# Another fixed order of the attention's tasks in front of a top-1 mixture of experts

## The chip, the cores and the metric

The kernel runs on one core of one Trainium2 chip. The metric is the device time of one execution in microseconds. A core has five engines that run their own instruction streams in order: TensorE (PE, with its weight loads shown apart as PEld), VectorE (DVE), ScalarE (ACT), GpSimd (POOL) and SyncE (SP, which issues transfers). They wait for one another through semaphores.

## The reference, cut to what matters

Causal softmax attention and a linear memory read-out, mixed by a gate per head (B=4 batches, H=8 heads, S=576 positions, D=64), are followed by a mixture of experts in which each of the 2304 tokens goes to one of 8 experts.

```python
scores = scale * np.matmul(q, k.transpose(0, 1, 3, 2))        # causal, softmax over the last axis -> a
local = np.matmul(a, v)
q_p = phi(q)                                                  # elu(q) + 1
mem_out = einsum(q_p, M_prev) / (einsum(q_p, z_prev) + 1e-06)
attn = g * mem_out + (1 - g) * local                          # g = sigmoid(beta), one per head
x = attn.transpose(0, 2, 1, 3).reshape(B * S, H * D)          # 2304 tokens of 512
e_idx = np.argmax(x @ w_gate, axis=1)                         # top-1 routing
for e in range(8):
    mask = e_idx == e
    out[mask] = gate_w[mask] * eom[mask, e] * (np.maximum(x[mask] @ w1[e], 0) @ w2[e])
```

## The kernel before

The attention works on 16 pairs of heads (g = 0 to 15, four pairs to a batch) and on five query tiles of each pair (qt = 0 to 4, the last of 64 rows). What it does to them is cut into 1181 named tasks, each bound to one engine. The function `job` writes them down; a string, `ORDER`, lists all 1181 names in a fixed order, and one loop issues them in that order. Each engine then does its own tasks strictly in the order in which it got them, and waits where the inputs of the next are not there yet. A few tasks may run on either of two engines: the copies out of PSUM and the casts carry `:ACT` or `:DVE` behind their name.

The names that the text needs, with the line at which the profile shows them:

- **SS** scores of a pair and query tile on PE (L570, for the last tile L557, `s` and `sd`); **M** mask and row maximum on DVE (L628, for the last tile L596, `st` and `nm`); **E** exponentials on ACT (L633, for the last tile L605, followed by a read of the accumulated row sum).
- **T** transposes of the probabilities on PE (L645, L614 and L616, into `pt`); **V** copies of them to SBUF (L492, `PT`), on ACT or DVE; **P** probabilities times values on PE (L680, `po`); **O** copies of these to SBUF (L492, `oT`), on ACT or DVE.
- **C** and **R** split query and key into a high and a low part (L461 ACT or DVE, L465 POOL). **ME**, **N1**, **N2** are the memory product (PE L736), its norm and its scaling (DVE L742, L743, L749); **MW** and **MC** its weights (PE L700, DVE L705).
- **PL** with **YL**, **XL** (PE L904, DVE L912 and L913, POOL L923) mix both parts for the last batch, half of the heads at a time. **RT**, **RK**, **Tgate**, **GP**, **GS**, **CA**, **CJ**, **CB**, **Tpos** are the routing of a batch: small reductions on DVE (L256 to L329 and L884 to L891), a ranking by matmul (PE L235 to L238, `rk`), a transpose of the gates (PE L308) and its copy (DVE L312). **Z** tasks prepare the weights of the expert that runs first (among them DVE L1002, PE L1062, ACT L1072).

PSUM holds four buffers for scores, two for transposes (`pt`) and two for everything else, so a transpose into `pt` also waits until the V copy of the one before the last is done. Behind the loop over `ORDER` the code is the same in both kernels: the last routing steps and the first expert's gemms, then the experts, from about 216 us to the end.

Of the kernel before, what the change touches and what calls it, by code (L numbers as in the profile page):

```python
# [54 lines left out]
T1_2_0 V1_2_0:ACT T1_2_1 M2_0_0 M2_0_1 M2_1_1 E2_0_1 TS0_0 F03 P0_256_0 V1_2_1:DVE E2_0_0 E2_1_1 T1_4 M1_3_1 F21 V1_4_0:ACT LM1 M2_1_0 M1_3_0 P0_256_1
C3:DVE F12 P1_0_0 E2_1_0 V1_4_1:DVE T2_0 load4 E1_3_0 E1_3_1 V2_0:DVE SS2_2 R3 M2_2_0 M2_2_1 O0_256:ACT O1_0:ACT SS2_3 T2_1 T1_3_1 load_v3 E2_2_0
V2_1:ACT M2_3_0 V1_3_1:ACT TS1_0 E2_3_0 SS2_4 T1_3_0 V1_3_0:ACT M2_3_1 MW1 F13 F04 E2_2_1 T2_2_0 T2_3_0 TS1_1 ranks M2_4_0 P1_256_0 C4:DVE E2_3_1 F22 MC1
V2_2_0:ACT SS3_1 M3_0_0 V2_3_0:ACT P1_256_1 T2_2_1 M3_1_0 M2_4_1 E2_4 V2_2_1:ACT E3_0_0 load5 F23 O1_256:DVE M3_0_1 T2_3_1 TS2_0 load6 E3_0_1 E3_1_0
V2_3_1:DVE SS3_2 ME0_0 M3_2_1 T2_4 E3_2_1 R4 M3_1_1 wgz V2_4_0:ACT N10_0 N20_0 V2_4_1:ACT F06 SS3_4 T3_2_1 T3_0 M3_2_0 ME0_1 F14 V3_0:ACT M3_4_0
V3_2_1:ACT SS4_1 M3_4_1 E3_2_0 N10_1 SS4_2 E3_1_1 N20_1 T3_1 T3_2_0 C5:ACT P2_0_0 P2_256_0 TS2_1 E3_4 M4_0_0 V3_1:ACT M4_0_1 F24 M4_2_1 G0_1 M4_2_0  # L60
V3_2_0:ACT O2_0:ACT E4_0_1 E4_0_0 T3_4 M4_1_1 E4_1_1 E4_2_1 P2_256_1 V3_4_0:DVE TS3_0 M4_1_0 O2_256:DVE T4_0 SS3_3 E4_1_0 load_v4 E4_2_0 V3_4_1:DVE
M3_3_0 ME0_4 C6:ACT V4_0:ACT T4_2_0 SS4_4 V4_2_0:ACT R5 N10_4 T4_2_1 R6 TS3_1 N20_4 M3_3_1 M4_4_0 V4_2_1:ACT T4_1 E3_3_0 M4_4_1 load7 E3_3_1 V4_1:ACT
ME0_3 SS4_3 E4_4 T3_3_1 V3_3_1:ACT T3_3_0 N10_3 V3_3_0:ACT N20_3 M4_3_0 F16 E4_3_0 M4_3_1 ME0_2 N10_2 TS4_0 F05 SS5_1 SS5_2 N20_2 F26 T4_4 M5_0_0
M5_0_1 E4_3_1 P3_0_0 V4_4_0:DVE P3_256_0 O3_0:ACT E5_0_0 load9 P4_0_0 E5_0_1 M5_1_0 G0_3 P3_256_1 load_v5 F15 C7:ACT M5_2_0 W0 O3_256:ACT T4_3_0
O4_0:ACT F07 V4_4_1:DVE F25 E5_1_0 R7 T4_3_1 PV0_2 M5_2_1 M5_1_1 PV0_1 SS5_4 V4_3_1:ACT E5_1_1 E5_2_1 V4_3_0:DVE T5_0 Y0_2 G0_4 V5_0:ACT E5_2_0 Y0_1
M5_4_0 SS5_3 G0_0 M5_4_1 LT0_0 load8 XD0_1 LC0_0:DVE T5_2_0 V5_2_0:ACT XD0_2 M5_3_1 T5_1 PV0_4 E5_4 M5_3_0 T5_2_1 SS6_2 SS6_1 V5_2_1:DVE F09 V5_1:ACT
E5_3_0 E5_3_1 Y0_4 OUT0_2 M6_0_0 LT0_1 F08 M6_2_1 LC0_1:ACT T5_4 load_v7 OUT0_1 E6_0_0 V5_4_0:ACT F19 M6_2_0 LM2 LS0 SS6_4 TS5_1 V5_4_1:ACT TS5_0
E6_2_1 F17 M6_1_0 TS4_1 T5_3_1 T5_3_0 LY0 XD0_4 M6_0_1 E6_0_1 LB0 G0_2 V5_3_1:ACT V5_3_0:ACT PV0_0 P4_256_0 M6_1_1 T6_2_1 F18 LA0 RT0_0 Y0_0 E6_1_1
E6_1_0 RT0_1 T6_0 SS7_1 XD0_0 P4_256_1 P5_256_0 O4_256:ACT V6_0:ACT V6_2_1:DVE M6_4_0 RT0_2 E6_2_0 C8:ACT R8 F27 RT0_3 RT0_4 M7_0_0 P5_0_0 P5_256_1
OUT0_4 T6_1 CA0 F28 E7_0_0 O5_0:ACT M6_4_1 E6_4 O5_256:DVE T6_2_0 load_v6 V6_2_0:ACT M7_0_1 M7_1_1 ME1_0 SS6_3 M7_1_0 SS7_3 load_v8 V6_1:ACT load10  # L70
# [4 lines left out]
F010 TS7_0 V7_4_0:ACT E8_1_0 F111 T8_0 N11_3 E8_2_0 GA0 N21_3 TS7_1 F110 V7_4_1:ACT M8_2_1 G1_1 M8_3_1 P6_256_0 E8_2_1 P7_0_0 P6_256_1 M8_3_0 V8_0:DVE
SS9_1 O6_256:ACT E8_3_1 F013 O7_0:DVE T8_2_1 T8_1 F210 V8_2_1:ACT F211 M9_0_0 M9_0_1 PV1_0 T8_2_0 E8_3_0 V8_1:ACT P7_256_0 Tgate40 M9_1_1 W1 E9_0_1
V8_2_0:ACT Y1_0 M9_1_0 XD1_0 P7_256_1 load12 E9_0_0 T8_3_0 O7_256:ACT G1_4 G1_3 E9_1_1 V8_3_0:ACT PV1_1 OUT1_0 E9_1_0 F113 CJ0 LM3 load_v9 PV1_2
T8_3_1 Y1_1 Y1_2 SS8_4 M8_4_0 T9_0 M8_4_1 PV1_3 LT1_0 C11:ACT V8_3_1:ACT XD1_1 SS9_3 SS9_2 E8_4 V9_0:ACT G1_2 Y1_3 OUT1_1 M9_3_1 M9_3_0 load_v10 R11
LT1_1 XD1_2 T9_1 V9_1:ACT E9_3_0 SS9_4 LC1_0:DVE LC1_1:DVE LS1 TS8_0 XD1_3 M9_2_1 T8_4 E9_3_1 M9_2_0 LY1 V8_4_0:ACT SS10_1 LB1 OUT1_3 RK0 Tpos10
V8_4_1:ACT OUT1_2 T9_3_1 E9_2_1 PV1_4 LA1 M10_0_0 T9_3_0 Y1_4 RT1_0 V9_3_1:ACT M10_0_1 T9_2_1 E9_2_0 RT1_1 Tpos20 M9_4_0 V9_2_1:ACT C12:ACT P8_256_0  # L80
P8_0_0 Tpos30 M10_1_1 M10_1_0 P8_256_1 Tpos40 M9_4_1 RT1_2 CB0 F213 E10_0_1 V9_3_0:ACT T9_2_0 E10_0_0 E10_1_0 V9_2_0:ACT O8_0:DVE T10_0 E9_4 RT1_3
E10_1_1 V10_0:ACT O8_256:DVE RT1_4 SS10_2 M10_2_1 M10_2_0 E10_2_1 SS10_3 TS9_1 ME2_0 M10_3_0 R12 N12_0 load_v11 RX1 T10_1 SS10_4 SEL0_3 V10_1:ACT
E10_3_0 SEL0_2 ZI T9_4 N22_0 V9_4_0:ACT G2_0 TS9_0 E10_2_0 ME2_3 M10_3_1 SS11_1 C13:ACT V9_4_1:DVE E10_3_1 N12_3 R13 XD1_4 T10_2_1 T10_3_0 N22_3
V10_3_0:DVE M10_4_0 M11_0_0 E11_0_0 V10_2_1:ACT P9_256_0 P9_0_0 P9_256_1 M11_1_0 O9_0:ACT TS8_1 G2_3 T10_2_0 load15 O9_256:ACT T10_3_1 OUT1_4 F015
M10_4_1 V10_2_0:ACT M11_0_1 V10_3_1:ACT M11_1_1 Tgate11 Tgate31 E11_1_0 E10_4 E11_0_1 E11_1_1 SEL0_1 ME2_1 N12_1 SS11_3 N22_1 SS11_4 T10_4 RK1
V10_4_0:ACT MW3 T11_0 M11_4_0 Tpos11 M11_3_0 load14 TS10_1 V10_4_1:ACT V11_0:ACT MC3 T11_1 M11_3_1 V11_1:ACT ME2_4 Tpos21 CA1 CJ1 CB1 SS11_2 M11_4_1
E11_4 SS12_1 E11_3_1 N12_4 N22_4 T11_4 ZC M11_2_1 E11_3_0 TS11_1 M11_2_0 Z1 Z2 Tpos31 load_v12 M12_0_0 Z3 Z4 G2_1 V11_4_0:DVE Z5 P11_0_0 TS11_0
O11_0:ACT P10_256_0 P10_0_0 P10_256_1 F115 Tpos41 Z6 Z7 E12_0_0 Tgate21 M12_0_1 Z8 Z9 Z10 V11_4_1:DVE O10_0:ACT O10_256:DVE TS10_0 T11_3_0 T11_3_1
V11_3_1:DVE E11_2_1 M12_1_0 M12_1_1 ZN ME2_2 E12_0_1 C14:ACT N12_2 V11_3_0:ACT Tgate41 N22_2 E11_2_0 SS12_3 W2 T11_2_1 V11_2_1:ACT T11_2_0 SEL1_3
SS12_4 E12_1_0 PV2_1 T12_0 load_v14 V11_2_0:ACT E12_1_1 V12_0:ACT M12_3_1 M12_3_0 F215 P11_256_0 G2_2 SEL1_4 M12_4_0 Y2_1 E12_3_1 E12_3_0 SS13_1  # L90
P11_256_1 M12_4_1 SEL1_2 T12_1 M13_0_0 T12_3_1 M13_1_0 O11_256:ACT M13_0_1 V12_1:ACT M13_1_1 E12_4 XD2_1 PV2_4 PV2_3 R14 Y2_4 E13_1_1 T12_3_0 E13_0_1
SS12_2 SS13_3 XD2_4 OUT2_1 OUT2_4 V12_3_1:ACT V12_3_0:DVE M12_2_1 G2_4 E13_1_0 GA1 E13_0_0 T12_4 Y2_3 V12_4_0:ACT E12_2_1 F014 LT2_0 M12_2_0 LT2_1
T13_0 F012 SEL1_1 XD2_3 V12_4_1:DVE T13_1 LC2_0:DVE LC2_1:ACT V13_0:DVE M13_3_0 LS2 E12_2_0 V13_1:ACT SS13_2 T12_2_0 T12_2_1 E13_3_0 V12_2_1:ACT LY2
P12_0_0 M13_3_1 TS12_0 SEL0_4 load_v13 V12_2_0:ACT M13_2_0 O12_0:ACT PV2_0 LB2 M13_2_1 E13_2_0 SS13_4 T13_3_0 PV2_2 Y2_0 F112 F114 T13_2_0 Y2_2
# [1709 lines left out]
```

## Time and profile before

| | |
|---|---|
| time, median of 3 runs | 468.69 us (468.49 to 468.74) |
| profiled execution | 468.34 us, of which its span is 466.3 us |
| granted TensorE clock, mean of the span | 0.996 |
| busy in the span | PE 456.7, PEld 354.8, DVE 284.9, ACT 262.4, POOL 271.1 us |
| the attention's tasks | from the start to about 202 us |
| experts | about 216 us to the end |

Busy time of PE counts pipelined matmuls with modelled ends, so 98% is not PE at its peak. An engine that waits and is not the last link of the chain costs nothing.

### The profile page before, as it was taken

The page shows a single profiled execution, that of the slowest core. Times are in us where ns is not written, and L with a number is a line of the kernel's source. Part 1 is how long each engine was busy: PE and PEld are TensorE (multiplying, and loading weights), DVE is VectorE, ACT ScalarE, POOL GpSimd, SP SyncE. Part 2 cuts the span into 40 slices and gives each one's busy share as a digit, 9 for nine tenths or more (in the row PEclk, how much of TensorE's full clock was granted, in tenths as well). Part 3 has the DMA queues.
Part 4 walks back from the last instruction along what each step waited for, and adds up shares of the span by engine and source line. Part 5 has one row for each costly group of instructions (what it writes and reads, how often), then busy time and mean ns, then how long its engine had stood idle before and what let it go on. Part 6 is the DMA issues. An engine that isn't in the chain of part 4 may idle for free.

```text
span 466.3 us, 10798 instructions
## 1 busy us (share of the span) xinstructions
PE 456.7 (98%) x3517; PEld 354.8 (76%) x3517; DVE 284.9 (61%) x851; ACT 262.4 (56%) x625; POOL 271.1 (58%) x274
## 2 busy tenths in 40 slices
...
GB/s 239 204 144 143 21 216 158 158 58 199 30 153 30 86 181 99 59 142 153 47 265 324 299 309 170 328 46 346 265 202 341 115 208 221 124 147 182 29 31 39
DMA packets 30119, 75.90 MB, mean 163 GB/s; under 512 B 4307, under 2 KB 4839, under 8 KB 30058
## 3 DMA queue, kind: packets, MB, share of 16 engines
...
## 4 chain that ended last, share of the span: by engine, by line
PE 88%; DVE 3%; issue 2%; POOL 2%; ACT 2%; DVEq 1%; POOLq 0%; ACTq 0%
PE py L1432 18%; PE h L1432 17%; PE po L680 10%; PE pt L645 8%; PE s L570 7%; PE me L736 4%; PE hp L1458 3%; PE cy L1601 3%; PE ch L1601 3%; PE sd L557 3%; PE pt L614 2%; PE px L1400 2%; PE he L1123 1%; PE pv L799 1%; PE pl L904 1%
## 5 line engine op out<-in xcount | busy, mean ns | idle before, releaser
L633 ACT ACTIVATE st<-st,nm 128x128 f32<-128x128 f32 (+3 forms) x128 | 71.4, 562 | 3.7 <-DVE nm L628 3.6
L1465 POOL TENSOR_TENSOR hl<-hT,hh 128x512 fp32r<-128x512 f32 x32 | 43.5, 1380 | 40.6 <-ACT hh L1464 40.5
L628 DVE CUSTOM_DVE_ANT_0 st<-s,mask 128x128 f32<-128x128 f32 (+3 forms) x128 | 58.2, 483 | 8.2 <-PE s L570 4.1
L1108 DVE CAST whi<-kept 128x1024 fp32r<-128x1024 f32 x32 | 26.0, 811 | 51.6 <-ACTq L1439 40.7
L465 POOL TENSOR_TENSOR lo<-qk,hi 128x1216 fp32r<-128x1216 f32 x15 | 42.1, 2805 | 24.7 <-ACT hi L461 19.5
L1111 DVE TENSOR_TENSOR wlo<-kept,whi 128x1024 fp32r<-128x1024 f32 x32 | 54.4, 1701 | 1.1
L492 ACT COPY PT<-pt 128x512 f32<-128x512 f32 (+2 forms) x89 | 45.2, 523 | 15.9 <-PE pt L645 13.8
L1432 PE MATMUL h<-whi,xh 128*128 (+1 forms) x136 | 53.9, 396 | 0.0
L1432 PE MATMUL h<-whi,xl 128*128 (+1 forms) x136 | 53.4, 393 | 0.0
L1432 PE MATMUL h<-wlo,xh 128*128 (+1 forms) x136 | 53.4, 392 | 0.0
L1432 PE MATMUL py<-whi,hh 128*128 (+1 forms) x128 | 51.9, 406 | 0.0
L1432 PE MATMUL py<-whi,hl 128*128 (+1 forms) x128 | 50.2, 392 | 0.3 <-POOL hl L1465 0.3
L1432 PE MATMUL py<-wlo,hh 128*128 (+1 forms) x128 | 50.2, 392 | 0.0
L680 PE MATMUL po<-PT,v 128*64 128x320 f32 (+4 forms) x480 | 49.1, 349 | 0.8 <-ACT oT_hT L492 0.4
L645 PE MATMUL pt<-ident,st 128*128 128x128 f32 x320 | 48.0, 280 | 0.4 <-ACT st L633 0.4
L1464 ACT CAST hh<-hp 128x512 fp32r<-128x512 f32 x32 | 19.1, 598 | 50.6 <-PE py L1432 50.6
L1445 ACT ACTIVATE h<-h 128x1024 f32<-128x1024 f32 x17 | 17.5, 1029 | 47.9 <-PE h L1432 47.9
L680 PEld LDWEIGHTS po<-PT,v 128*64 128x64 f32 x480 | 29.6, 137 | 17.7 <-issue 2.8
L1411 POOL TENSOR_TENSOR xl<-x,xh 128x512 fp32r<-128x512 f32 x16 | 21.7, 1358 | 34.3 <-issue 19.0
L645 PEld LDWEIGHTS pt<-ident,st 128*128 128x128 f32 x320 | 35.2, 142 | 7.8 <-ACT st L633 2.5
...
L1432 PEld LDWEIGHTS h<-whi,xh 128*128 128x128 f32 x136 | 25.5, 188 | 6.0 <-ACT h L1445 0.3
...
## 6 DMA issues: line engine op xcount, KB each, us to landing
...
```

What stands on the lines that cost most here:

```text
L465: G.tensor_tensor(c["lo"][:, TQ:], c["raw"][:, TQ:], f32(c["hi"])[:, TQ:], op=ALU.subtract)
L492: (A.copy if e == "ACT" else V.tensor_copy)(dst(), src())
L570: T.matmul(c()["ss", q][j], l[r, lc], m[r, KC:KC + w], start=(a == 0), stop=(a == 2))
L628: V.tensor_tensor_reduce(st[:, :w], c()["ss", qt][j], mask[:, 512 - w:512], -SCALE, 3.0e38, ALU.add, ALU.min, negm()[:, i:i + 1])
L633: A.activation(st, st, AF.Exp, bias=c()["negm"][:, i:i + 1], scale=-1.0, accum_out=sums()[:, qt, 2 * p + j:2 * p + j + 1])
L645: T.transpose(pt[:, (m * k1 + i) * P:(m * k1 + i + 1) * P], st[:, i * P:(i + 1) * P], ident)
L680: T.matmul(po[64 * j:64 * j + 64, qs - q0:q1 - q0], vt[:, k, 64 * j:64 * j + 64], PT[:, j, k, qs:q1], start=(k == 0), stop=(k == kn - 1))
L1108: join((A.copy if eng is A else eng.tensor_copy)(whi[:, e % 2, c, :], raws[e, c]))
L1111: join(eng.tensor_tensor(wlo[:, e % 2, c, :], raws.pop((e, c)), f32(whi[:, e % 2, c, :]), op=ALU.subtract))
L1432: i = T.matmul(o[n % nh], l[:, z], m[:, n * 512 + part.start:n * 512 + part.stop], start=(c == 0 and k == 0 and n < nh), stop=(c == 3 and ...
L1465: G.tensor_tensor(hl[:, z], hT[:, z], f32(hh)[:, z], op=ALU.subtract)
L1601: i = apart(T.matmul(o[w * q:w * q + w], x[:, z:z + w], wide[b][:, m + size * q:m + size * q + size], start=(j == 0), stop=(j == len(todo) ...
```

## The change

The string `ORDER` is replaced by another order of the same 1181 tasks; no task is added, removed or altered. It was looked for by a search that lengthens tasks at random and lets two-operand tasks of VectorE and GpSimd exclude each other. The first row of the string and the start of its second are the same; behind them a name stands 7.7 places from where it stood, on average. 48 tasks change between ACT and DVE: 26 go from DVE to ACT and 22 from ACT to DVE, so that ACT has 140 of these tasks in place of 136 and DVE 44 in place of 48. Two rows of the string, before and after:

```diff
-E7_1_1 RX0 N11_0 E7_0_1 C9:ACT T6_4 N21_0 V6_4_0:ACT E7_1_0 PV0_3 M6_3_1 E6_3_1 M6_3_0 P6_0_0 Y0_3 V6_4_1:DVE TS6_0 E6_3_0 T7_0 O6_0:DVE M7_3_0 M7_3_1
-R9 TS6_1 V7_0:ACT SS7_2 ME1_4 N11_4 E7_3_0 T6_3_1 T7_1 E7_3_1 SS7_4 V7_1:ACT N21_4 M7_2_0 Tgate10 E7_2_0 V6_3_1:ACT M7_2_1 ME1_2 G1_0 N11_2 SS8_1
+SS7_3 load10 N21_0 RX0 T6_4 C9:ACT M7_3_0 TS6_0 M6_3_1 PV0_3 V6_4_0:ACT V6_4_1:DVE R9 Y0_3 P6_0_0 E7_0_1 T7_0 TS6_1 E6_3_1 M7_3_1 O6_0:ACT M6_3_0
+T6_3_1 E7_1_0 E7_1_1 V6_3_1:ACT E7_3_1 Tgate10 ME1_4 N11_4 SS7_2 N21_4 T7_1 SS7_4 V7_1:ACT M7_2_1 M7_2_0 ME1_2 V7_0:ACT SS8_1 E7_3_0 F29 T7_3_0 N11_2
```

In these rows T6_3_1 stood behind SS7_2 and ME1_4 on PE; now it stands directly behind T7_0.

**ACT, 188 to 191 us.** The rows are ACT's around the copy of `pxe` (task ZY, four rows). Before:

```order
L633 ACTIVATE st15_3_0_3209,sums3_2473<-st15_3_0_3209,nm15_3003 128x512
L492 COPY PT0_127<-pt14_2_0_3243 128x3x128
L1072 COPY star0_2910<-pxe_3252 128x128
...
L1072 COPY star3_3160<-pxe_3252 128x128
L492 COPY PT0_127<-pt14_2_1_3226 128x3x128
L492 COPY oT3_hT_2774<-po15_512_3271 128x64
L492 COPY oT3_hT_2774<-po15_0_3284 128x128
L633 ACTIVATE st15_2_0_3241,sums3_2473<-st15_2_0_3241,nm15_3003 128x384
```

Now:

```order
L492 COPY PT0_127<-pt14_2_0_3220 128x3x128
L492 COPY PT1_128<-pt15_1_0_3230 128x2x2x128
L1072 COPY star0_2979<-pxe_3252 128x128
...
L1072 COPY star3_3166<-pxe_3252 128x128
L633 ACTIVATE st15_2_0_3248,sums3_2465<-st15_2_0_3248,nm15_3000 128x384
L492 COPY oT3_hT_2780<-po15_512_3273 128x64
L633 ACTIVATE st15_2_1_3250,sums3_2465<-st15_2_1_3250,nm15_3000 128x384
L633 ACTIVATE st15_3_0_3269,sums3_2465<-st15_3_0_3269,nm15_3000 128x512
L492 COPY oT3_hT_2780<-po15_128_3298 128x128
```

The copies V14_2_1 (`pt14_2_1`) and O15_0 (`po15_0`) have left ACT for DVE. On PE the product P15_128, which writes over the buffer that O15_512 reads, stood directly behind P15_0 and P15_512; now four matmuls of 320 columns (P14_256, first part) stand between.

**DVE, 134 to 136 us.** The rows are DVE's around M11_4 (L596, `st11_4`), whose exponential feeds the transpose T11_4. Before:

```order
L628 ISA st11_3_1_2363,nm11_2231<-s11_3_1_2303,mask_138 128x512
L628 ISA nm11_2231 128x1
L323 TENSOR_REDUCE ps1_2347<-pos1_2346 128x5
L884 TENSOR_REDUCE addc1_2377<-oha_85 128x8
L887 TENSOR_TENSOR cnt_90<-cnt_90,addc1_2377 128x8
L891 CAST cntb_91<-cnt_90 128x8
L596 ISA st11_4_2344,nm11_2231<-sd11_4_1_2317,maskd_139,nm11_2231 128x288
```

Now:

```order
L320 TENSOR_TENSOR pos1_2339<-rk1_2325,oha_85 128x40
L596 ISA st11_4_2332,nm11_2228<-sd11_4_1_2303,maskd_139,nm11_2228 128x288
L596 ISA nm11_2228 128x1
L705 COPY mz3_1867<-mw3_2334 64x4x16 x2
L628 ISA st11_3_1_2356,nm11_2228<-s11_3_1_2192,mask_138 128x512
L628 ISA nm11_2228 128x1
L323 TENSOR_REDUCE ps1_2340<-pos1_2339 128x5
L884 TENSOR_REDUCE addc1_2364<-oha_85 128x8
```

M11_4's second half now stands ahead of M11_3_1 and of the routing's counting (L323, L884, and L887 and L891 further down).

**PE and DVE, 194 to 199 us.** PE's rows of the last pair's transposes, before:

```order
L308 MATMUL gp0_3337<-ident_77,og0_1540 5x128
L645 MATMUL pt15_3_0_3339<-ident_77,st15_3_0_3209 128x128 x4
L904 MATMUL pl0_1_3351<-rzt_136,oT3_hT_2774 128x160 x2
L645 MATMUL pt15_3_1_3354<-ident_77,st15_3_1_3267 128x128 x4
L308 MATMUL gp1_3369<-ident_77,og1_2278 5x128
L645 MATMUL pt15_2_0_3371<-ident_77,st15_2_0_3241 128x128 x3
```

Now, with DVE's rows of the same place behind them:

```order
L308 MATMUL gp0_3339<-ident_77,og0_1497 5x128
L904 MATMUL pl0_1_3347<-rzt_136,oT3_hT_2780 128x160 x2
L645 MATMUL pt15_3_0_3355<-ident_77,st15_3_0_3269 128x128 x4
L645 MATMUL pt15_3_1_3364<-ident_77,st15_3_1_3309 128x128 x4
L308 MATMUL gp1_3371<-ident_77,og1_2276 5x128
L645 MATMUL pt15_2_1_3381<-ident_77,st15_2_1_3250 128x128 x3
```

```order
L913 TENSOR_TENSOR yl0_1_3373<-pl0_1_3347,rr3_3141 128x320
L270 SCALAR_TENSOR_TENSOR oha_85<-mx2_3352,wt2_3362 128x40
L492 COPY PT1_128<-pt15_3_1_3364 128x4x128
L286 TENSOR_TENSOR wt2_3362<-lg2_2099,oha_85 128x40
L312 COPY gs1_3385<-gp1_3371 5x128
```

The product PLl0_1 (`pl0_1`) now comes directly behind GP0, without T15_3_0 between them, and the copy V15_3_1 (`PT1<-pt15_3_1`), which ACT did, is now DVE's, between L270 and L286.

## Rows read from the trace of the kernel before

**Rows 1.** The page: busy time, share of the span and instructions of each engine.

```profile
PE 456.7 (98%) x3517; PEld 354.8 (76%) x3517; DVE 284.9 (61%) x851; ACT 262.4 (56%) x625; POOL 271.1 (58%) x274
```

**Rows 2.** Busy time by stretch: bounds and length in us, engines, granted clock, DMA.

```profile
70.00:100.00 30.00, 30.00 (x308) 23.48 (x307) 27.21 (x104) 26.66 (x73) 17.27 (x15) 1.00 0.36 122
...
195.00:200.00 5.00, 4.38 (x54) 3.60 (x52) 4.83 (x27) 2.63 (x7) 2.33 (x4) 1.00 0.20 56
...
sum 193.00, PE 191.73 PEld 150.54 DVE 167.81 ACT 156.16 POOL 114.65; mean PE 17.43 PEld 13.69 DVE 15.26 ACT 14.20 POOL 10.42
```

**Rows 3.** PE's waits, whole span: line, releaser, us in total, times, longest.

```profile
PE po L680 <- ACT oT_hT L492: 0.4, 1, 0.4
PE pt L645 <- ACT st L633: 0.4, 1, 0.4
PE s L570 <- DVE nm L628: 0.3, 1, 0.3
PE py L1432 <- POOL hl L1465: 0.3, 1, 0.3
PE po L680 <- DVE gs L312: 0.3, 1, 0.3
PE rk L235 <- DVE oha L270: 0.2, 1, 0.2
```

**Rows 4.** Timeline, 188 to 190 us: start, us, instruction [idle before, its releaser].

```profile
188.71 0.77 ACT L1072 COPY star<-pxe 128x128 f32<-128x128 f32 x4 [0.75 <-PE pxe L1062]
...
189.34 0.53 ACT L492 COPY PT<-pt 128x384 f32<-128x384 f32 x1
...
189.71 0.44 ACT L492 COPY oT_hT<-po 128x64 f32<-128x64 f32 x2
...
190.03 0.55 PE L680 MATMUL po<-PT,v 128*64 128x128 f32 x6 [0.41 <-ACT oT_hT L492]
```

**Rows 5.** Timeline, 134 to 137 us.

```profile
134.81 0.22 DVE L884 TENSOR_REDUCE addc<-oha 128x8 f32<-128x40 bf16 x1
...
135.34 0.51 DVE L596 CUSTOM_DVE_ANT_0 st<-sd,maskd,nm 128x288 f32<-128x288 f32 x1
...
135.98 0.78 ACT L605 ACTIVATE st<-st,nm 128x576 f32<-128x576 f32 x1 [1.09 <-DVE nr L742]
...
136.90 0.20 PEld L614 LDWEIGHTS pt<-ident,st 128*128 128x128 f32 x2 [0.22 <-ACT st L605]
```

**Rows 6.** Timeline, 138 to 139 us: the weight load of P10_256.

```profile
138.56 0.74 PEld L680 LDWEIGHTS po<-PT,v 128*64 128x64 f32 x8 [0.32 <-DVE zw L1002]
```

**Rows 7.** Timeline, 195 to 199 us: the end of the attention.

```profile
195.57 0.57 PEld L904 LDWEIGHTS pl<-rzt,oT_hT 128*128 128x128 f32 x4 [0.35 <-DVE yl L913]
...
196.22 0.60 PE L645 MATMUL pt<-ident,st 128*128 128x128 f32 x4
...
197.41 0.74 POOL L923 TENSOR_TENSOR xa<-x,yl 128x256 f32<-128x256 f32 x1 [1.08 <-DVE yl L913]
...
197.47 0.73 DVE L286 TENSOR_TENSOR wt<-lg,oha 128x40 f32<-128x40 f32 x1
...
198.13 0.27 DVE L312 COPY gs<-gp 5x128 f32<-5x128 f32 x1
...
198.46 0.55 PE L680 MATMUL po<-PT,v 128*64 128x128 f32 x6 [0.27 <-DVE gs L312]
```

**Rows 8.** Timeline, 81 to 83 us: around T7_0.

```profile
81.44 0.58 ACT L492 COPY PT<-pt 128x512 f32<-128x512 f32 x1
...
82.41 0.72 ACT L633 ACTIVATE st<-st,nm 128x512 f32<-128x512 f32 x1
82.46 0.44 PE L645 MATMUL pt<-ident,st 128*128 128x128 f32 x2
```

**Rows 9.** DVE's copies of `pt`, whole span: ns min/median/max, first and last start.

```profile
L492 DVE COPY PT<-pt x23: 406/681/693, 9.4 to 178.8; 128x512 f32<-128x512 f32 x13, 128x256 f32<-128x256 f32 x5, 128x384 f32<-128x384 f32 x5
```

More of the change, by code (lines that the diff above doesn't have):

```diff
@@ L55 @@
[L55 to L70, printed above, removed]
@@ L75 @@
[L75 to L90, printed above, removed]
@@ L91 @@
[L91 to L94, printed above, removed]
@@ L103 @@
-P15_512_0 fetch4 P15_0_0 TL2_0 G3_0 O15_512:ACT O15_0:ACT P15_128_0 P14_256_0 E15_2_0 O15_128:DVE E15_2_1 P14_256_1 TL0_0 W3_1_1 W3_1_2 PLl1_1 LA2
-E15_3_1 W3_1_3 O14_256:ACT YLl1_1 XLl2_0 PLl4_1 PLl3_0 YLl4_1 GP0 T15_3_0 TL1_1 V15_3_0:ACT XLl1_1 XLl4_1 TL4_1 YLl3_0 PLl0_1 T15_3_1 GS0 RT2_0 GO0
-RT2_1 RT2_2 RT2_3 GP1 T15_2_0 YLl0_1 RT2_4 Tgate12 GS1 V15_3_1:ACT OL4 RX2 GO1 RK2 V15_2_0:ACT CA2 Tpos12 Tgate32 Tpos22 Tgate22 CJ2 T15_2_1 Tpos32
-Tgate42 V15_2_1:ACT GA2 CB2 Tgate52 P15_384_0 O15_384:ACT P15_256_0 Tpos42 Tgate62 TL0_1 TL3_0 XLl3_0 XLl0_1 PLl3_1 G3_3 SEL2_0 OL1 O15_256:ACT SEL2_3
```

68 lines of the change are left out of this document (54 added, 14 removed).

## The prediction

> **What bounds the kernel now.** I read the page's first part, then busy time by stretch, then PE's waits, and last the timeline at each place where something starts late. The page has PE busy for 98% of the span, every other engine for 76% or less [rows 1]. In the attention, which is all that the change touches, PE is busy 191.73 of the 193.00 us from 12 to 205 us [rows 2]; the one stretch where it is not is 195 to 200 us, with 4.38 of 5.00, where the last pair's work runs out and little is left to fill gaps. PE's waits of the whole span, as far as the view names them, are six of 0.2 to 0.4 us, 1.9 us in all, one of which (L1432, 0.3 us) lies in the experts, behind the change [rows 3]. So the order can win about 1.6 us of listed waits, and lose as much as it likes. Behind the attention PE goes on without a listed wait up to that one of L1432, so a microsecond won or lost before 202 us should arrive at the end.
>
> A wait that the matmul side does not list can still be there: PE's busy time has modelled ends, so a short wait is covered by the end of the matmul before it. The weight loads show such places; I use them as bounds.
>
> **What the change does.** The same instructions run, so PE's work is the same; only waits, and the changes of tile shape, can differ. I went through PE's rows in the new order, and for each counted what its releaser's engine has ahead of it. Four places carry the sum.
>
> *P15_128 at 190 us.* It writes into the buffer that the copy O15_512 reads. On ACT that copy stood behind the four rows of ZY (from 188.71) and V14_2_1 (0.53 us from 189.34), so it began at 189.71 and PE started at 190.03 after a wait of 0.41 [rows 4]. Now V14_2_1 is on DVE and PE has four matmuls of P14_256 ahead of P15_128. An exponential has taken V14_2_1's place ahead of the copy, so the copy is about as late as before; the gain comes from the four matmuls. Their price is not in these rows apart, but six matmuls of 128 columns take 0.55 there, so four wider ones are at least 0.37 us (estimate). Between nothing (the copy is later still) and the whole wait of 0.41 and a little that the modelled end covers, 0.6, I take −0.45.
>
> *T11_4 at 137 us.* Its releaser is the exponential E11_4, which began at 135.98, after M11_4's second half on DVE (135.34, 0.51 us); ahead of that DVE did L884 (0.22 us from 134.81) and two more small rows, 134.81 to 135.34, 0.53 us in all [rows 5]. These rows now stand behind M11_4, and so does M11_3_1. The load wait is 0.22 us [rows 5] and the two waits of this kind in the list are 0.4 and 0.3 [rows 3]. Bounds 0 and −0.7, taken −0.4, the longer of the listed ones.
>
> *P10_256 at 139 us.* Its load waited 0.32 us for Z2 on DVE [rows 6], with no matmul wait listed. In the new order Z2 is no longer the last to come. Bounds 0 and −0.32, taken −0.15.
>
> *T6_3_1 at 83 us, a new wait.* SS7_2 and ME1_4 no longer lie between T7_0 and T6_3_1. By the old times T7_0's second transpose is done about 82.46 + 2 x 0.11 = 82.68, with 0.11 us a transpose from 196.22, where four take 0.60 with a modelled end and the next row of PE came 0.43 us later [rows 7, 8]. The exponential E6_3_1 has a copy (0.58 from 81.44) and one exponential of a 128-column tile ahead of it, which with its overlap takes about what the 256-column one took there, since both leave its start near 82.41; it lasts 0.72 [rows 8], so it would be done near 83.1: 0.45 us late. If ACT comes to this place earlier than before, nothing is late. Bounds 0 and +0.5, taken +0.25.
>
> *The end, 195 to 199 us.* PLl0_1 waited for YLl3_0 with T15_3_0 in front of it, and its load still showed 0.35 us [rows 7]. Now T15_3_0 comes behind it, so its four transposes, 0.43 us, no longer cover: +0.43 there. But those transposes then fall behind, into the room of the waits that followed: RK2's for L270 (0.2, [rows 3]) and P15_384's for the copy GS1 (0.27, at 198.46, [rows 7]). GS1 itself hangs on DVE. There L286 took 0.73 us from 197.47, most of it beside POOL's L923 (197.41 to 198.15) [rows 7]; the copy V15_3_1 (up to 0.69 us, [rows 9]) now goes ahead of it. If L286 was merely held up by POOL's addition, the copy fills the hold, L286 runs in a short time once POOL is done, and GS1 starts where it did, near 198.13. If not, GS1 comes 0.69 later. The Trainium skill, "SBUF — State Buffer", section "Who interferes with whom", says that a VectorE instruction with two SBUF inputs contends with a GpSimd instruction that reads SBUF and that the loser blocks fully, while one with at most one SBUF input does not; by that the hold is real and the place costs nothing, and without it the sum below would be 0.5 us worse. I go by the row, since L286 ended within 0.05 us of POOL's end. Bounds −0.3 (both later waits filled) and +0.5, taken +0.1.
>
> *Small things.* At other places I count short waits that go (ME3_0 behind ZR, the ME tasks of batch 1) and short ones that come (P6_256, T12_3_1, T15_2_1 for its `pt` buffer); no row shows any of them as a PE wait, so they lie between −0.6 and +0.6, taken −0.35, as I count more that go. PE has two changes of tile shape fewer, at the most a transpose's slot each, 0 to −0.2, taken −0.1.
>
> The 48 tasks that change engine cost nothing where neither engine is waited for: ACT was busy 156.16 and DVE 167.81 of 193.00 us [rows 2]. A copy of 512 columns takes 0.58 on ACT [rows 8] and up to 0.69 on DVE [rows 9]; ACT gets four such tasks more. The cover is ACT's idle time, which was 3.3 us of 30 between 70 and 100 us [rows 2].
>
> Sum: −0.45 − 0.4 − 0.15 + 0.25 + 0.1 − 0.35 − 0.1 = **−1.1 us**. The profiled execution took 468.34 us, 2.0 us more than its span and 0.35 less than the median of 468.69; I take the difference from the median, 467.6 us. A difference under 0.2%, 0.94 us, is about what a measurement can't tell from none.
>
> **The rivals.**
> - *The waits are given back: same, 468.5.* PE is so nearly without waits that any order will have a few late inputs of its own. For it: T6_3_1, and PLl0_1 without cover, are new waits that I can already point at. If only the terms with listed waits at 190 and 137 us go (−0.85) and the new ones come larger than taken (+0.5 at T6_3_1, its upper bound, and +0.25 at the end, half of its bound), the change is −0.1; with the small things in balance at −0.1 it is −0.2. Against it: the waits that go are measured, and the new ones only counted.
> - *ACT falls behind between 70 and 100 us: slower, 469.9.* ACT is busy 26.66 of 30 us there [rows 2]. If the four copies that it got, 4 x 0.58 = 2.3 us, fall in this stretch and the exponentials run late by more than the transposes' lead, PE loses what ACT can't catch up. It decides from the point where this stretch's idle time of 3.3 us no longer lies where the added copies do; with 2.3 us lost and the 1.1 won it ends at 468.69 + 1.2 = 469.9. Against it: DVE has 2.8 us idle in that stretch too, and tasks move both ways.
> - *PE is not the bound: faster, 466.* The weight loads are busy only 150.54 of 193.00 us [rows 2], so 42 us could hide starved PE time that the modelled ends cover, and then an order can win several microseconds. With twice the short waits that I count gone, −2.5 us, it is 466.2. The Trainium skill, "Perfetto Trace Analysis", section "Identifying the Most-Contended Engine", says that matmul busy share is no good measure of how near TensorE is to its limit, and names the share of the weight loads instead; by that TensorE has 22% of headroom here. Against it: a transpose every 0.11 us keeps its pace through most of the attention.
> - *The order does not do what it was looked for.* Two-operand tasks kept apart would shorten DVE rows like L286; if DVE is not waited for at those places, nothing comes of it. That is inside "same".
>
> **How the numbers follow.** The forecast, that the sum holds within what its terms leave open to the better side, −0.9 to −1.8 us, has 0.40; given back in part or in whole, −0.9 to +0.9, 0.38; slower through ACT, above +0.94, 0.14; PE not the bound, below −1.8, 0.08. The forecast's own range is 466.9 to 467.8. The first and the last case are faster by over 0.2%: faster 0.48, same 0.38, slower 0.14. The range leaves out the lower end of the last case and the upper part of the slower one, 2 in 10 together: 466.5 to 469.4.
>
> **What would show it.** PE without a wait at P15_128 and T11_4; T6_3_1's load released by ACT's exponential, late by up to 0.5 us; PLl0_1's load wait near 0.8; L286 of the third batch short, behind a copy; the experts' first L1432 about 1 us earlier than 216.4. The prediction is wrong if PE's list names waits at places not above, if ACT's idle time between 70 and 100 us is gone while PE loses there, or if the experts start earlier and the end does not.

## The result: 1.1% slower, and on more than one level

| | time, us, median (range, runs) | ratio, 95% interval |
|---|---|---|
| before | 468.59 (468.41 to 468.74, 4) | |
| changed | 473.79 (472.06 to 476.30, 4) | 1.0111 (1.0075 to 1.0148) |

The forecast was 467.6 in a range of 466.5 to 469.4. The changed kernel's four runs fall into two groups, 472.06 and 472.08, and 475.50 and 476.30, where before's lie within 0.33 us. The profiled execution is one of 472.06, with a span of 470.3 us.

The page's first part of the changed kernel, as [rows 1], and two of its stretches and their sum, as [rows 2]:

```profile
PE 457.7 (97%) x3517; PEld 355.6 (76%) x3517; DVE 287.5 (61%) x847; ACT 263.4 (56%) x629; POOL 271.5 (58%) x274
```

```profile
40.00:70.00 30.00, 28.38 (x293) 21.52 (x291) 25.97 (x86) 26.14 (x72) 20.19 (x17) 1.00 0.33 112
70.00:100.00 30.00, 29.72 (x298) 23.74 (x298) 27.39 (x105) 26.61 (x74) 15.54 (x14) 1.00 0.41 134
...
195.00:200.00 5.00, 4.38 (x34) 3.34 (x30) 4.16 (x19) 1.36 (x5) 2.18 (x4) 1.00 0.03 7
...
sum 193.00, PE 189.87 PEld 150.16 DVE 170.07 ACT 156.49 POOL 115.34; mean PE 17.26 PEld 13.65 DVE 15.46 ACT 14.23 POOL 10.49
```

From 12 to 205 us TensorE is busy 189.87 us in place of 191.73, and the stretch that lost most, 40 to 70 us, is one of which the prediction says nothing. ScalarE between 70 and 100 us is as full as before (26.61 against 26.66). TensorE's waits, as [rows 3], with the one before the first score left out:

```profile
PE pt L645 <- ACT st L633: 1.8, 2, 1.4
...
PE rk L235 <- DVE oha L270: 0.8, 1, 0.8
PE pl L904 <- DVE yl L913: 0.5, 1, 0.5
PE s L570 <- DVE nm L628: 0.3, 1, 0.3
PE py L1432 <- POOL hl L1465: 0.3, 1, 0.3
PE h L1432 <- POOL xl L1411: 0.3, 1, 0.3
PE pt L645 <- ACT PT L492: 0.2, 1, 0.2
```

4.2 us in seven lines, against 1.9 in six. Two are new and large: 1.4 us for an exponential and 0.8 us for the routing's `oha`. The timeline of the changed kernel from 58 to 63 us shows the first of them from its root, in the order of time:

```profile
58.39 2.76 POOL L465 TENSOR_TENSOR lo<-qk,hi 128x1216 fp32r<-128x1216 f32 x1 [0.86 <-ACT hi L461]
...
58.86 2.91 DVE L520 SCALAR_TENSOR_TENSOR phi<-qk,phi 128x576 f32<-128x576 f32 x1
...
61.70 0.28 DVE L628 CUSTOM_DVE_ANT_0 st<-s,mask 128x128 f32<-128x128 f32 x1
...
62.07 0.40 ACT L633 ACTIVATE st<-st,nm 128x128 f32<-128x128 f32 x1 [1.90 <-DVE nm L628]
...
62.62 0.33 PE L645 MATMUL pt<-ident,st 128*128 128x128 f32 x1 [1.40 <-ACT st L633]
```

F25 (L520, the last step of elu(q) + 1 for pair 5; both operands lie in SBUF) came up on VectorE 0.47 us after GpSimd had begun R7 (L465). It took 2.91 us, where L520 otherwise takes 0.75, and was done 0.62 us after R7. I call that a hold: an instruction stays unfinished until another engine's is done. Behind F25 on VectorE stood M5_0_0 (61.70), whose exponential (62.07) feeds the transpose T5_0 on TensorE (62.62). In the old order F25 went first, from 58.84 to 59.57, and R7 ran its 2.85 us from 59.38. Before, from 58 to 60 us:

```profile
58.84 0.73 DVE L520 SCALAR_TENSOR_TENSOR phi<-qk,phi 128x576 f32<-128x576 f32 x1
...
59.38 2.85 POOL L465 TENSOR_TENSOR lo<-qk,hi 128x1216 fp32r<-128x1216 f32 x1 [2.91 <-ACT hi L461]
```

The second wait looks the same, at the last ranking:

```profile
206.50 1.47 DVE L270 SCALAR_TENSOR_TENSOR oha<-mx,wt 128x40 bf16<-128x40 f32 x1
206.51 1.40 POOL L923 TENSOR_TENSOR xa<-x,yl 128x256 f32<-128x256 f32 x2
...
208.03 0.19 PE L235 MATMUL rk<-oha,upper 128*128 128x40 bf16 x1 [0.84 <-DVE oha L270]
```

L270 takes 0.19 us alone, and took 0.55 at this place in the old order. Where the time went, read from TensorE's rows of both traces: GP0 came 2.57 us later (197.32 against 194.75), GP2 2.81 (204.34 against 201.53), the last ranking 3.65 (208.03 against 204.38), the first L1432 3.65 (220.03 against 216.38), and the span is 4.0 longer. Of the 2.57, 0.56 were there before the two orders differ (T0_3_1 at 12.31 against 11.75 us); two further profiles of the same kernel have that row at 12.14 and 11.72, so it is no part of the change.

### The profile page after: what moved, and what is told of

Read it like the earlier page. It is cut to its first block, busy times and chain, and to the rows that moved or that the text cites. A ratio compares the mean times of both kernels' runs of the same rounds, so it can differ in the third digit from the quotient of the medians.

```text
span 470.3 us, 10802 instructions
## 1 busy us (share of the span) xinstructions
PE 457.7 (97%) x3517; PEld 355.6 (76%) x3517; DVE 287.5 (61%) x847; ACT 263.4 (56%) x629; POOL 271.5 (58%) x274
## 4 chain that ended last, share of the span: by engine, by line
PE 83%; DVE 7%; ACT 4%; issue 2%; POOL 1%; DVEq 1%; POOLq 0%; ACTq 0%
PE py L1432 18%; PE h L1432 18%; PE po L680 7%; PE pt L645 7%; PE s L570 6%; PE me L736 4%; PE hp L1458 3%; PE cy L1601 3%; PE ch L1601 3%; ACT st L633 2%; PE sd L557 2%; PE pt L614 2%; PE px L1400 2%; PE pl L904 1%; DVE st L628 1%
## 5 line engine op out<-in xcount | busy, mean ns | idle before, releaser
L633 ACT ACTIVATE st<-st,nm 128x128 f32<-128x128 f32 (+3 forms) x128 | 71.4, 560 | 7.5 <-DVE nm L628 6.9
L1108 DVE CAST whi<-kept 128x1024 fp32r<-128x1024 f32 x32 | 30.1, 940 | 55.8 <-ACTq L1439 43.9
L628 DVE CUSTOM_DVE_ANT_0 st<-s,mask 128x256 f32<-128x256 f32 (+3 forms) x128 | 58.3, 483 | 7.8 <-PE pt L645 3.2
L465 POOL TENSOR_TENSOR lo<-qk,hi 128x1216 fp32r<-128x1216 f32 x15 | 42.6, 2843 | 21.4 <-ACT hi L461 15.7
L1432 PE MATMUL h<-whi,xh 128*128 (+1 forms) x136 | 53.8, 396 | 0.0
L1432 PE MATMUL h<-whi,xl 128*128 (+1 forms) x136 | 53.4, 393 | 0.3 <-POOL xl L1411 0.3
L1432 PE MATMUL h<-wlo,xh 128*128 (+1 forms) x136 | 53.4, 393 | 0.0
L1432 PE MATMUL py<-whi,hh 128*128 (+1 forms) x128 | 51.9, 405 | 0.0
L645 PE MATMUL pt<-ident,st 128*128 128x128 f32 x320 | 48.8, 282 | 2.7 <-ACT st L633 1.8
L1432 PE MATMUL py<-whi,hl 128*128 (+1 forms) x128 | 50.2, 392 | 0.3 <-POOL hl L1465 0.3
L1432 PE MATMUL py<-wlo,hh 128*128 (+1 forms) x128 | 50.2, 392 | 0.0
L1111 DVE TENSOR_TENSOR wlo<-kept,whi 128x1024 fp32r<-128x1024 f32 x32 | 48.1, 1503 | 1.1
L680 PEld LDWEIGHTS po<-PT,v 128*64 128x64 f32 x480 | 31.2, 137 | 17.0 <-issue 1.9
L645 PEld LDWEIGHTS pt<-ident,st 128*128 128x128 f32 x320 | 34.8, 142 | 11.7 <-ACT st L633 4.8
L513 POOL TENSOR_SCALAR phi<-qk 128x576 f32<-128x576 f32 x16 | 26.6, 1668 | 8.7 <-DMA qk<-in_qk 5.9
```

What stands on the lines that cost most here:

```text
L465: G.tensor_tensor(c["lo"][:, TQ:], c["raw"][:, TQ:], f32(c["hi"])[:, TQ:], op=ALU.subtract)
L628: V.tensor_tensor_reduce(st[:, :w], c()["ss", qt][j], mask[:, 512 - w:512], -SCALE, 3.0e38, ALU.add, ALU.min, negm()[:, i:i + 1])
L633: A.activation(st, st, AF.Exp, bias=c()["negm"][:, i:i + 1], scale=-1.0, accum_out=sums()[:, qt, 2 * p + j:2 * p + j + 1])
L645: T.transpose(pt[:, (m * k1 + i) * P:(m * k1 + i + 1) * P], st[:, i * P:(i + 1) * P], ident)
L680: T.matmul(po[64 * j:64 * j + 64, qs - q0:q1 - q0], vt[:, k, 64 * j:64 * j + 64], PT[:, j, k, qs:q1], start=(k == 0), stop=(k == kn - 1))
L1108: join((A.copy if eng is A else eng.tensor_copy)(whi[:, e % 2, c, :], raws[e, c]))
```

## The experiments

**Theory A**: the new order lets a VectorE task with two SBUF operands come up while GpSimd is at a long one of its own; it is held to the end of it, and where TensorE needs what stands behind it, time is lost. A race of a few tenths of a microsecond decides at one place which goes first, hence the levels. **Theory B**: ScalarE, or VectorE as a whole, became too full, or TensorE's own sequence is worse. Each group of runs shares a chip with runs of before, whose medians were 468.74, 469.06, 469.11 and 469.03.

**F25 moved behind Y0_1**

```diff
-... V4_4_1:ACT F25 M5_0_0 E5_0_0 M5_2_0 O3_256:ACT R7 T4_3_0 E5_2_0 PV0_1 Y0_1 T5_0 ...
+... V4_4_1:ACT M5_0_0 E5_0_0 M5_2_0 O3_256:ACT R7 T4_3_0 E5_2_0 PV0_1 Y0_1 F25 T5_0 ...
```

> The new order with one task moved: F25 (L520, VectorE, two operands in SBUF) stands behind Y0_1 instead of ahead of M5_0_0, so that it starts when GpSimd's R7 (L465, 2.8 us) is over. In the changed kernel F25 took 2.91 us beside R7, and TensorE waited 1.40 us at T5_0. Theory A (the two instructions exclude each other, and the wait at T5_0 is that hold): F25 near 0.75 us, no wait of over 0.5 us at T5_0, time 1.4 to 2 us under the new order's faster runs, near 470.3. Theory B (ScalarE or VectorE is too full there whatever F25 does): the wait moves behind F25 to the next transposes, and the time stays within 0.5 us of the new order.

Measured: 472.09 (six runs: 469.96; 472.05, 472.08 and 472.09; 473.32 and 473.38), ratio 1.0071 (1.0049 to 1.0092). The profile, of a run of 472.08, from 60 to 64 us and from 34 to 40 us:

```profile
60.42 2.78 POOL L465 TENSOR_TENSOR lo<-qk,hi 128x1216 fp32r<-128x1216 f32 x1 [0.87 <-ACT hi L461]
...
63.09 0.38 PE L645 MATMUL pt<-ident,st 128*128 128x128 f32 x2
...
63.89 0.75 DVE L520 SCALAR_TENSOR_TENSOR phi<-qk,phi 128x576 f32<-128x576 f32 x1
64.06 1.73 POOL L807 TENSOR_TENSOR xd<-x,y 128x512 f32<-128x512 f32 x1 [0.85 <-DVE y L803]
```

```profile
33.96 2.76 POOL L465 TENSOR_TENSOR lo<-qk,hi 128x1216 fp32r<-128x1216 f32 x1
34.35 3.22 DVE L520 SCALAR_TENSOR_TENSOR phi<-qk,phi 128x576 f32<-128x576 f32 x1
...
39.69 0.63 PE L614 MATMUL pt<-ident,st 128*128 128x128 f32 x4 [1.61 <-DVE PT L492]
```

F25 is short and T5_0 waits for nothing; this time GpSimd was the one held (L807, 1.73 us in place of 1.28). So the wait of 1.40 us was the hold, and B's wait behind it did not come. Of the time, though, A's expectation missed: the median is that of the new order's faster runs, and only 469.96 is near 470.3. The trace shows why: it has another hold, F23 by R4, with T2_4 waiting 1.61 us for a copy behind it. TensorE's order is the same in both kernels, so each matmul can be set beside itself. From 37 to 41 us this trace loses 2.2 us against the profile of 472.06, and from 62 to 65 us it gains 2.0: F25's hold is worth 2.0 us of TensorE, and F23's takes it away again.

**The new order again**, unchanged, twice.

> The new order unchanged. Its four runs lay at 472.1 twice and at 475.5 and 476.3. Theory A (starts within some 0.1 us of each other decide which of two excluding instructions goes first, so the order has several outcomes): again two or more levels, 472 and 475 to 476, and in a profile of the higher level a further VectorE or GpSimd instruction stretched by 1 us or more and a TensorE wait behind it. Theory B (a disturbance of the chip in two runs): all runs near 472.

> The new order unchanged, for another look at its levels: Theory A: a profile near 472.1 shows F23 at 0.75 us, one at 474.2 or more shows F23 near 3.2 us; where it is above 475 a third change must show, in the granted clock or a third hold.

Measured: 474.15, 474.81, 475.77 and 475.91; then 474.62 and 471.93. Profiles came from 474.81 and 474.62. The first, from 34 to 41 us, and the same place in the profile of 472.06 under it:

```profile
34.33 2.76 POOL L465 TENSOR_TENSOR lo<-qk,hi 128x1216 fp32r<-128x1216 f32 x1
34.72 3.22 DVE L520 SCALAR_TENSOR_TENSOR phi<-qk,phi 128x576 f32<-128x576 f32 x1
...
40.05 0.52 PE L614 MATMUL pt<-ident,st 128*128 128x128 f32 x3 [1.61 <-DVE PT L492]
```

```profile
34.42 0.76 DVE L520 SCALAR_TENSOR_TENSOR phi<-qk,phi 128x576 f32<-128x576 f32 x1
34.42 0.80 POOL L531 COPY sums<-sumd 64x1 f32<-64x1 f32 x1
35.19 2.78 POOL L465 TENSOR_TENSOR lo<-qk,hi 128x1216 fp32r<-128x1216 f32 x1
```

At 472.06 F23 came first, held a small copy of GpSimd's (L531, 0.80 us; 0.18 alone), and R4 followed. At 474.81 R4 had been running for 0.39 us and F23 took 3.22; the profile of 474.62 is the same (R4 at 34.14, F23 3.22 us from 34.54). The difference in when the two come up is under 1 us, and what hangs on it is 2.5 us of time; matmul by matmul, both traces lose 2.2 us against that of 472.06 between 37 and 41 us. That is the level at 474 to 475. The runs above 475 had a lower mean granted clock, 0.992 to 0.993 against 0.999 for the profiled 474.81, and left no profile.

**The old order with F25 late**

```diff
-... V4_4_1:DVE F25 E5_1_0 R7 T4_3_1 PV0_2 M5_2_1 M5_1_1 ...
+... V4_4_1:DVE E5_1_0 R7 T4_3_1 PV0_2 M5_2_1 F25 M5_1_1 ...
```

> The old order with one task moved: F25 stands behind M5_2_1 instead of ahead of it, so that it comes up for issue some 0.2 to 0.5 us after R7 has started. Theory A: F25 is held until R7 ends, 2.5 us or more in place of 0.73, TensorE waits 0.8 to 1.8 us within 5 us of it, time 469.5 to 470.5 against 468.6. Theory B (only a task 0.75 us later, with no hold): within 0.3 us of the old order.

Measured: 470.86 (470.74 to 471.29, 5 runs) against 468.74, ratio 1.0046 (1.0033 to 1.0059), 2.1 us slower from one task moved by one place on VectorE. The timeline:

```profile
59.43 2.79 POOL L465 TENSOR_TENSOR lo<-qk,hi 128x1216 fp32r<-128x1216 f32 x1 [2.90 <-ACT hi L461]
60.40 2.43 DVE L520 SCALAR_TENSOR_TENSOR phi<-qk,phi 128x576 f32<-128x576 f32 x1
...
63.23 0.50 PE L570 MATMUL s<-lo,hi 64*128 64x512 f32 x1 [0.71 <-DVE nm L628]
```

F25 ended 0.61 us after R7, as it did in the new order. A holds; B is out. Within 5 us the list names three waits of TensorE, 1.2 us together (0.71, 0.23 and 0.27), and the time is a little above the 469.5 to 470.5 expected. TensorE's order is that of before, and the same matmuls come 0.05 us later than before at 60 us, 1.2 at 63, and 2.3 from 68 on to the last one: the whole loss arises in these 8 us, and the list names about half of it. It also shows that nothing else of the new order is needed for such a loss.

**C4 behind F23 alone**, so that R4 can't start before F23:

```diff
-... V2_3_0:DVE C4:DVE F22 MC1 ... O1_256:ACT F23 M3_0_1 ...
+... V2_3_0:DVE F22 MC1 ... O1_256:ACT F23 C4:DVE M3_0_1 ...
```

> The new order with the cast C4 behind F23 and F25 left where it is, so that only the hold of F25 remains. Theory A (the new order's levels are the race of F23 with R4, and the levels above 475 are that stall and what TensorE's clock does behind it): F25 held near 2.9 us in every run, one level of 471.8 to 472.8, no run above 473.5. Theory B (levels above 475 have a cause of their own): runs of 475 and more still come up.

Measured: 472.55 (472.30 to 473.14, 5 runs), ratio 1.0075 (1.0061 to 1.0089). The profile, of the run of 473.14, from 33 to 36 us and from 58 to 63 us:

```profile
33.72 0.76 DVE L520 SCALAR_TENSOR_TENSOR phi<-qk,phi 128x576 f32<-128x576 f32 x1
...
58.88 2.92 DVE L520 SCALAR_TENSOR_TENSOR phi<-qk,phi 128x576 f32<-128x576 f32 x1
...
62.65 0.44 PE L645 MATMUL pt<-ident,st 128*128 128x128 f32 x2 [1.42 <-ACT st L633]
```

F23 is short, F25 is held, and no run is above 473.2: the level at 474 to 475 is the hold of F23. Two of the five runs lie at 473.11 and 473.14, the others at 472.30 to 472.55; in the profiled 473.14 TensorE also waited 1.3 us for `hl` (L1432, in the experts), in place of 0.3 in the profile of 472.06. The runs above 475 are not settled by this. None of these five had a low clock (0.995 at the least), but among 29 runs of the old order two had 0.992 and lay at 470.73 and 471.03, against a median of 469.06; in the old order's profile F23 begins 1.4 us ahead of R4 and is not held. Those two left no profile, but it is unlikely that the low clock needs this hold.

**Both moved**

> The new order with both of its holds taken out: F25 behind Y0_1, as in the run before, and the cast C4 (VectorE) behind F23, so that GpSimd's R4, which waits for C4, can't start before F23. The trace of the new order's higher level showed F23 held for 3.22 us by R4, which had started 0.39 us earlier, and TensorE waiting 1.61 us at T2_4; in its lower level F23 went first. Theory A (the levels are this race): one level, within 0.5 us, near 470.0, the fastest run of the kernel with F25 alone moved. Theory B (the levels have another cause): runs still at 472 and above. Either way TensorE's waits at T6_1, T6_3_1 and PLl0_1, 1.3 us together, stay, so this is not expected to reach 468.7.

Measured: 470.15 (469.29 to 471.51, 12 runs) against 469.06, ratio 1.0020 (1.0007 to 1.0034). The profile, of a run of 470.07, from 33 to 38 us, and its waits:

```profile
33.49 0.76 DVE L520 SCALAR_TENSOR_TENSOR phi<-qk,phi 128x576 f32<-128x576 f32 x1
34.17 0.79 DVE L461 CAST hi<-qk 128x1216 fp32r<-128x1216 f32 x1
35.10 2.79 POOL L465 TENSOR_TENSOR lo<-qk,hi 128x1216 fp32r<-128x1216 f32 x1 [0.81 <-DVE hi L461]
```

```profile
PE rk L235 <- DVE oha L270: 0.8, 1, 0.8
PE pl L904 <- DVE yl L913: 0.5, 1, 0.5
PE pt L645 <- ACT st L633: 0.4, 1, 0.4
PE py L1432 <- POOL hl L1465: 0.3, 1, 0.3
PE s L570 <- DVE nm L628: 0.3, 1, 0.3
PE h L1432 <- POOL xl L1411: 0.3, 1, 0.3
PE pt L645 <- ACT PT L492: 0.2, 1, 0.2
```

The new order's median lay 5.2 us over before's; this lies 1.1 us over, so the two holds were about 4.1 us; by TensorE's rows they are 2.0 and 2.2. Of the 1.1 that are left, the listed waits, 2.8 us against before's 1.9, would account for 0.9.

**T15_3_0 put back ahead of PLl0_1**, on top of that:

```diff
-... YLl3_0 PLl0_1 GS0 RT2_0 GO0 T15_3_0 RT2_1 ...
+... YLl3_0 T15_3_0 PLl0_1 GS0 RT2_0 GO0 RT2_1 ...
```

> The last kernel, with T15_3_0 put back ahead of PLl0_1 on TensorE. Theory A (the prediction's term: the product lost its cover): the wait of 0.71 us there falls to about 0.3, and 0.3 to 0.4 us less time than without it, near 469.6. Theory B (what follows is bound by VectorE's chain to the ranking, which this doesn't move): the wait moves to T15_2_1 or the ranking and the time stays.

Measured: 469.94 (469.38 to 470.91, 11 runs), ratio 1.0016 (1.0007 to 1.0025), no difference that can be told from 470.15; one of 0.3 us could not be told either, so the times don't decide. The rows speak for B: the wait at L904 is gone from the list, and the matmuls behind PLl0_1 come 0.7 us earlier, but the ranking RK2 and T15_2_1 behind it lose 0.7 again, each waiting for VectorE.

**The last two additions apart**, twice:

```diff
-... SEL2_2 O15_256:ACT SEL2_4 SEL2_1 PLl2_1 YLl3_1 YLl2_1 XLl3_1 XLl2_1 GP2 ...
+... SEL2_2 O15_256:ACT PLl2_1 YLl3_1 YLl2_1 XLl3_1 SEL2_4 SEL2_1 XLl2_1 GP2 ...
```

> The new order with the last two GpSimd tasks of the attention apart: SEL2_4 and SEL2_1 stand between the additions XLl3_1 and XLl2_1, so that no addition runs when VectorE forms oha (L270) of the last batch, which took 1.47 us beside them in the changed kernel, while TensorE waited 0.84 us at the ranking. Theory A: L270 near 0.2 us, the wait at L235 gone, 0.6 to 0.9 us under the new order's faster runs. Theory B (L270 is late for another reason): the wait stays.

> The kernel with the last two additions apart, again, since its times spread from 471.5 to 477.7 and its one profile was of 471.5. Theory A (all levels come from the race of F23 with R4, plus what TensorE's clock does after the stall): a profile of 475 or more shows F23 held for over 3 us, a TensorE wait of 1.6 us at T2_4, and a lower granted clock in the stretch behind it. Theory B (moving the additions costs something of its own, in some runs): such a profile shows a new wait behind 200 us.

Measured: 475.85 (471.48 to 477.74, 6 runs) and 473.83 (470.93 to 475.23, 4 runs). Both profiles came from the lowest run, so the second question stays open. In both the wait for L270 is gone; in the first TensorE waited 1.0 us for `hl` (L1432 of the experts) in place of 0.3, in the second 0.3. With the levels on top, the times decide nothing. So the same edit was made without them:

> The new order with both early holds out (F25, C4 moved) and the last two additions apart, so that L270 is not held. Theory A (the wait of 0.84 us at the ranking is lost time): 0.7 to 0.9 us under the kernel with two holds out, near 469.3. Theory B (behind the ranking TensorE meets GpSimd's chain, as the kernel with the additions apart showed with a wait of 1.0 us at L1432 in place of 0.3): within 0.3 us of the kernel with two holds out.

Measured: 469.73 (468.95 to 470.35, 11 runs) against 469.11, ratio 1.0014 (1.0005 to 1.0023). That is 0.4 us under the kernel with two holds out, between A and B, and with this spread anything from nothing to 1 us. The two profiles decide it better. L270 took 0.24 us. TensorE's GP2 came 0.36 us later than in the kernel with two holds out (202.53 against 202.17), the ranking behind it 0.64 earlier (205.22 against 205.86), and the last matmul is still 0.76 earlier (460.93 against 461.69). So the hold of L270 was worth 1.0 us of TensorE, and the time gained arrives at the end: A.

Not every stretched row is out, however: three more of VectorE's are in every profile of the new order, this one too, and no run takes them out. In the profile of 472.06 they are L852 at 75.39 (1.31 us; about 0.2 before), L887 at 109.59 (1.14; 0.57 before) and L286 at 131.20 (1.74; 0.31 before), each beside an L807 or L465 of GpSimd. No TensorE wait is listed behind them; what they cost is not shown.

**The old order with two of the new order's gains**, then with two more of the kind:

```diff
-... M11_3_1 V11_1:ACT ME2_4 Tpos21 CA1 CJ1 CB1 SS11_2 M11_4_1 E11_4 ...
+... M11_3_1 V11_1:ACT ME2_4 M11_4_1 Tpos21 CA1 CJ1 CB1 SS11_2 E11_4 ...
-... V14_2_0:ACT PLl2_0 ZX YLl2_0 ZY XLl0_0 V14_2_1:ACT W3_1_0 ...
+... V14_2_0:ACT V14_2_1:DVE PLl2_0 ZX YLl2_0 ZY XLl0_0 W3_1_0 ...
```

```diff
-... ZC M11_2_1 E11_3_0 TS11_1 M11_2_0 Z1 Z2 Tpos31 ...   ZP M14_4_0 ZR ZG ...
+... ZC M11_2_1 Z1 Z2 E11_3_0 TS11_1 M11_2_0 Tpos31 ...   ZP ZR M14_4_0 ZG ...
```

> The old order with only two of the new order's gains: M11_4's second half ahead of the routing's counting on VectorE, and V14_2_1 on VectorE instead of ScalarE. Theory A (the prediction's two largest gains are real and additive): the waits at T11_4 (0.36 us) and P15_128 (0.41 us) are gone, time 0.6 to 0.8 us under the old order, near 468.0. Theory B (the experts' start is bound by GpSimd's chain of gathers, so that TensorE's earlier arrival is lost in a longer wait at L1432): the waits are gone and the time stays within 0.3 us.

> The old order with two more moves beside those two: Z1 and Z2 ahead of M11_2_0, and ZR ahead of M14_4_0 on VectorE. In the trace with two moves TensorE waited 0.4 us for Z2 at P10_256, and lost about 0.3 us around ME3_0, behind ZR. Theory A: both waits go, 0.5 to 0.7 us under the kernel with two moves, 1.3 us under the old order. Theory B (other inputs of the same tasks are as late): less than 0.2 us under the kernel with two moves.

Measured: 468.26 (467.55 to 469.23, 11 runs) against 469.06, ratio 0.9980 (0.9970 to 0.9990), and 467.96 (467.49 to 470.14, 12 runs) against 469.11, ratio 0.9978 (0.9969 to 0.9988). So the two moves together gain, 0.8 us by the medians. The rows place 0.3 of it, at P15_128. The first kernel's matmuls, in the order of before: T11_4 begins at 136.43 in place of 136.90, but P10_256 goes on at 138.53 in place of 138.56, since it now waits 0.37 us for Z2 instead; P15_128 begins at 189.69 in place of 190.03, and the last matmul is 0.33 us earlier. So the gain at T11_4 was lost 2 us later. Nor had there been a matmul wait at T11_4: the 0.36 us that the expectation puts there is a wait of T0_3, at 11.05 us, ahead of the place where the orders differ. The rest of the 0.8 is not placed; each profile is of one run. Before, the wait at 11 us:

```profile
11.05 1.36 PE L645 MATMUL pt<-ident,st 128*128 128x128 f32 x8 [0.36 <-ACT st L633]
```

The two further moves took the wait for Z2 away, but gave hardly more time (0.3 us between the medians, within the spread). The second kernel's profile, of a run of 468.71, shows where it can go:

```profile
226.68 1.04 POOL L1386 DMA_INDIRECT out<-ye,rowe  x1 [0.30 <-issue]
...
232.05 2.53 POOL L1465 TENSOR_TENSOR hl<-hT,hh 128x512 fp32r<-128x512 f32 x2 [4.33 <-DMA out<-ye,rowe]
...
233.37 0.50 PE L1432 MATMUL py<-whi,hl 128*128 128x512 f32 x1 [1.19 <-POOL hl L1465]
```

`hl` began 5.4 us after L1386, held by that transfer. In the traces of before, of the changed kernel, and of the kernels with F25 moved and with both moved it began after 3.8 us, released by ScalarE, and TensorE waited 0.3 us. Here the last matmuls came 0.9 us later for it. The same late transfer is in the profiles of 474.81 (new order), 471.48 (additions apart) and 473.14 (C4 alone), with TensorE waiting 1.0 to 1.3 us, so it can spread the times by about 1 us. Why it is late in some executions is open. This is the best version of the study, 0.2% faster than the old order.

## Why the prediction was wrong

The step that failed is the one under "What the change does": that only TensorE's inputs move, to be read off by counting what stands ahead of them on the releaser's engine, at the durations of before's trace. It holds for each engine taken alone. It leaves out that a duration depends on what another engine is doing at that moment. F25's row of before, 0.73 us, was no property of the instruction but of its place ahead of R7. The order moved it 0.5 us to the wrong side of R7's start; it took 2.91 us, and TensorE lost 2.0. F23's hold, in part of the runs, cost 2.2 more, and L270's 1.0. The prediction did see the mechanism, at L286, where it was to gain from it, and named no other pair; in its list of rivals the effect appears only as a gain that may not come (two-operand tasks kept apart). The rival that ended slower was put on ScalarE's load between 70 and 100 us, which did not change (26.61 us busy).

Point by point:
- **TensorE bounds the attention.** Right: its waits are what the time follows; 4.2 us listed against 1.9.
- **P15_128, T11_4 and P10_256** (−1.0 together). P15_128 is right: its wait is gone, and the move alone is worth 0.3 us in the old order's rows. T11_4 was misread: the two listed waits "of this kind", 0.4 and 0.3, are at 11.05 and 7.89 us, not at T11_4, and both lie ahead of the place where the orders differ, so the order could win 0.9 us of listed waits and not 1.6. T11_4's load wait of 0.22 was there and is gone, but in the old order its gain was lost at P10_256. P10_256 waits no more in the new order; no run tests that alone.
- **T6_3_1** (+0.25, released by an exponential). Right: its load waited 0.38 us for L633, at 86.54.
- **PLl0_1 without cover** (load wait near 0.8). Right: 0.74 us on the load side, 0.55 on the matmul side. **The end as a whole** (+0.1): from GP0 to GP2 it took 7.02 us in place of 6.78, +0.24.
- **L286 behind the copy**: it began at 200.51 and took 0.24 us, ending 0.05 after POOL's addition (199.97 to 200.70). Right. F25 and F23 agree, at full size, with the rule of the Trainium skill, "SBUF — State Buffer", section "Who interferes with whom", that was weighed there: each waited for the whole rest of GpSimd's instruction. F26, in the last section, does not: it took 0.97 us beside a GpSimd instruction that reads SBUF for 1.65, and there the measurement decides.
- **Small things** (−0.35). Not borne out, and the sum without holds has the wrong sign. With both early holds out the new order is still slower than the old by 0.20% (0.07% to 0.34%), some 1 us, where the sum was −1.1. Among what is new in that trace are the ranking's 0.8 us and the three waits of 0.2 to 0.5 at L904 and L645. With L270's hold out too, 0.6 us over the old order are left, 1.7 from the sum; where they arise is not shown, and the three stretched rows that stay are one candidate.
- **"PE is not the bound"**: the weight loads' busy share, from which that rival argued, stayed at 76% while the profiled span grew by 4.0 us, so it told nothing of this change.

What stays open: how the runs above 475 come to a lower mean clock, since none of them left a profile. It goes with the new order more often than with the old (4 of its 10 unchanged runs had 0.993 or less, and 2 of 29 of the old order beside one group), but it came in the old order too, where the profile has no hold of F23.
